# Three one-pass products of split operands in place of sums of fewer fp32 products, in the MLP of a recurrence-plus-MLP kernel

## The chip, the core and the metric

The kernel runs on one core of a Trainium2 chip. The metric is device time in microseconds, the median of the runs. Each core has five engines that work through queues of their own: TensorE (PE, its weight loads shown as PEld), VectorE (DVE), ScalarE (ACT), GpSimd (POOL) and SyncE (SP), which here starts nearly all DMA transfers. TensorE writes only to PSUM, eight banks of 128 x 512 fp32.

## What is computed

```python
def _attn_ref(q, k, v, alpha):            # 4 batches, 8 heads, 768 steps, 48 wide
    ...
    for t in range(S):
        state = alpha[:, :, t, :, None] * state + np.einsum('bhd,bhe->bhde', k[:, :, t], v[:, :, t])
        y[:, :, t] = np.einsum('bhd,bhde->bhe', q[:, :, t], state)
def _moe_ref(x, g_ln, w_ch1, w_ch2):      # x is y as (4, 768, 384)
    ...
    xn = (x - mu) / np.sqrt(var + 1e-06) * g_ln
    ch = np.maximum(xn @ w_ch1, 0.0) @ w_ch2      # 384 -> 1536 -> 384
    return (x + ch).astype(np.float32)
```

The reference's setup multiplies the weights by fp64 factors, so they arrive as 64-bit floats (12 pieces of 768 KB) and are turned into fp32 on the chip.

## The kernel before

**Chunks.** The 768 steps are cut into six chunks of 128 (c = 0 to 5) for each of four batches (b). `attention(c, b)` does the recurrence of one chunk and batch in matrix form: logarithms and exponentials of the sums of alpha (ACT), q and k scaled by them (L312, DVE), transposes on TensorE (L328 in fp32 for c below IN_HALVES = 2, else L349 as 16-bit halves), scores (L369 in chunk 0, L541 else), state updates (L399, L412, L414) and the output (L424 or L440). Then the layer norm: mean and square (L473), x normalised (L479 or L483), x transposed (L490 in fp32, L506 in halves) into xT.

**Weights.** `take_weights(i)` loads piece i (L211), turns it from 64-bit to fp32 with five DVE operations and one of ACT (L223 to L233), and starts the load of piece i + 3. Pieces 0 to 5 are w1, 6 to 11 are w2.

**MLP of chunk 0.** Plain fp32: `hidden` (L564, relu at L567) and `project` (L576).

**MLP of chunks 1 to 5.** A scheme with fewer products, made with sums of blocks, in the manner of Strassen. The first layer needs, for each of two rounds, 15 block products (`hidden_product`, L856, two matmuls of 256 columns each) where a plain one would need 18; the second layer needs 20 (`product`, L676, four matmuls of 192 columns each) where it would need 24. The price is sums: of weights (`combine_first` L805, `combine_weights` L636), of x (`combine_x` L830), of hidden blocks (`combine_hidden` L663), and one or more sums for each product that leaves PSUM (L860 to L899 and L683 to L745, on DVE, ACT, and on POOL as "late" sums such as L692, L881 and L891). The relu is L907 (ACT).

**Order.** The order of the work on all engines is written out by hand: each letter of ORDER takes one more step of one generator. Lower-case letters are `attention` of the 24 chunk-batch pairs, A to L the weight pieces, Y and Z `hidden` and P and Q `project` of chunk 0 (two batches each), M and V the products, S, W, X, N the sums, R the relus, digits loads and the shared matmuls, O the residual input. Each engine does its part in this order and waits where an input or a buffer is not ready.

Of the kernel before, what the change touches and what calls it, by code (L numbers as in the profile page):

```python
# [9 lines left out]
FP32 = mybir.dt.float32  # L10
INT32 = mybir.dt.int32
UINT32 = mybir.dt.uint32
# [7 lines left out]
IN_HALVES = 2  # L20
STAGED = 3

ORDER = (
    "0aa0bb00c2211dd2a3a2aabbbcaaacbbb0bd1a1abbbdfa1dddaaa3bbbec4aac2cd0baaafdAcbe2cc"
    "ffebdddccccdebb31eg0abhAffffeeecA4gdddccA5fdggheddeeeccYYiYhBjfcfhdgeeecggdchhhg"  # L30
    "hBB1ZZZfffB3CCZAefffe5hghB4fCjYYYYYiZZZCYYZZDD2jji3YYiDjjjhiiEZZZC0kDYYY3hhhZEig"
    "FFE5iggjGlF4ZZZZZgglS1lEHYYYhhghHjYYGYYhZZ2llgll3jHZFYGjHkkZkgI0kk0kjjjYZZnKI3i3"
    "ImQSSiiGii4n2jj1jSj5IlkkkkJKSSSSl1feeJn2eKeJLLnhL0hi02jSmPSPSjjmmQ1PPKSSSPkffPP1"
    "fnhPhSmkSWWSQ2SmmSefefWgnggnhQphSogSilllS5n3mimnggXXlXXX33WQQQ0nnXQXk4ppXXomSlll"
    "lnMMpmMoonMMMMMM2MMWSSkk0XSXlmmnnnmmMmMMM3MM13MnMnooppMMMoMMMMWpkrRM0M5poqooo4iq"
    "WWjjMMMMiMMRWMMMpooRiRMMMWMMoMMMlMMOOM1rrr22MMMRRqipMpoiikWMMMMRRMRMMMnnppokMMMM"
    "MRRRNNp3nMONlNlp0nnpWOqtrrmmNWNrN0MMNMMMMMNkNMMMMNN3MMsMMMMMmq0pNlpq1q3kMNOMlkMN"
    "MMMM5XXXXXrrrqq4MqqNXt1XoMMMMMMXXsstqqproM2MrrrJMMuvpoMMMMMMXMMMMMMXsMMMMMtMMrMo"
    "stssMMMqMtMtMM52rrsttssm4ssstMRttMMMMtt1MrMOOMMMMrMvMO2MMMMRRRvRMMMMMMMRRMMRMMML"
    "u31uMMRMRMMssNqNNNvrsmu22RNNNNNRqqNNNNm001MpMMMMMMMMMMM3MMMMMMMMMMMMNMMMrppNoNuv"  # L40
    "vMMoMMMMMXXX3MMM1XXvuu5vuuXvwXXvx4twuuvvqqMXXOOuMMsttttOMMMMMMMMMMXMMMwtMMMMwMMM"
    "33txxxMMMMMMMRqMMMMMMMMMMMMMMMussMsruuwrxRRRMMMMMRRRMRxMMRMMMMwwMMMMMMvxvvvvv5xx"
    "xwwwwwNNRONRRNttqqMMNNxMMMMMxNvMMMMMMMMNNNNNwwxsvMvwwMMxsMMuNNMMXXxNNxxxXXMXXXMM"
    "MXMMMMMXOMMMxMMXXMMMMMMMMMMwwOOuMMMMMMMMMMMMMMMMMMMMMMMMMMMRRRMMMMMMMMMMMROMxwuR"
    "uuwMMMMMMMMMMRRRRNRMMRRMMNMNNMNNNNMMMMMMMMMMMxNMNNXXXXXXMMMXNNMMMMMMNNNMMVVVVVVX"
    "MMMXXXMMMMMMMMVVVVVVVVOOOMOVVVVVVVVVVVVVVVRRRRRVVVVVVVVVRVVVVVVVVVVVVVVVVVVVVVVR"
    "RRNNRNRMMNRNNNMMMNNNMMMMNNNMMMMMMMMMMMMMMMMMMMNNMMMMNMMMMMMMM"
# [4 lines left out]
def kernel(  # L52
# [11 lines left out]

# [10 lines left out]
    NJ = DF // P  # L99
    assert S % P == 0 and H % 2 == 0 and D <= 64 and DM % P == 0 and DF % P == 0  # L100
    assert out.shape == (B, S, DM) and B * P <= 512 and DM + 2 * NP <= 512

    cpool = ctx.enter_context(tc.tile_pool(name="const", bufs=1))
    raw = ctx.enter_context(tc.tile_pool(name="raw", bufs=B // 2))
    stage = ctx.enter_context(tc.tile_pool(name="stage", bufs=STAGED))
# [6 lines left out]

    HS = P // 2
    halves = [slice(HS * s, HS * s + HS) for s in range(2)]
    raws = {}

# [10 lines left out]

    def loads(n):

        src = {"a": alpha, "k": k, "q": q}[n]  # L130
        lone = None
        for c in range(NCB):
            for m in range(B // 2):
                if c < 3:
                    t = raw.tile([P, 2, 2, NP, D], FP32, name=f"r{n}", tag="in", bufs=6)
                elif lone is None:
                    t = lone = raw.tile([P, 2, 2, NP, D], FP32, name=f"r{n}", tag="in", bufs=6)
                step = 2 if 0 < c < 3 else 1
                for i in ((0, 1) if c == 0 else (0,) if step == 2 else (1, 0)):
                    bs = slice(2 * m + i, 2 * m + i + step)  # L140
                    to = t[:, i:i + step].rearrange("t b i p d -> t b (i p d)")
                    if n != "a" or c == 0 or (step == 1 and i == 1):
                        nc.sync.dma_start(
                            to, src[bs, c * P:(c + 1) * P].rearrange("b t h d -> t b (h d)"))
                    else:
                        for h in range(2):
                            nc.sync.dma_start(to[halves[h], :1], of_pair(src, c, m, h)[:, :1])
                        if step == 2:
                            nc.sync.dma_start(to[:, 1], src[2 * m + 1, c * P:(c + 1) * P].rearrange(
                                "t h d -> t (h d)"))  # L150
                    raws.update({(n, c, 2 * m + j): t[:, j] for j in range(i, i + step)})
                    yield

    def loads_of_v():
        for c in range(NCB):
            for m in range(B // 2):
                bs, rows = slice(2 * m, 2 * m + 2), slice(c * P, (c + 1) * P)
                vn = raw.tile([P, 2, 2, NP, D], FP32, name="vn", tag="vn")
# [4 lines left out]
                if c:  # L163

                    vx = raw.tile([P, 2, NP, D], FP32, name="vx", tag="vx")
# [8 lines left out]
    mask, mask_of_halves = tri.bitcast(INT32), consts[:, 2 * P:2 * P + HS].bitcast(INT32)  # L174
# [15 lines left out]

    w1 = cpool.tile([P, NJ // 2, NF, 2 * P], FP32, name="w1")
    w2 = cpool.tile([P, NJ, DM], FP32, name="w2")
# [5 lines left out]
    for i in range(NJ // 2):  # L198
        cs, js = slice(2 * i * P, 2 * (i + 1) * P), slice(2 * i, 2 * (i + 1))
        pieces.append((w1[:, i], w1_src[:, :, cs]))  # L200
        pieces.append((w2[:, js], w2_src[:, js]))
# [770 lines left out]
```

## Time and profile before

| | us |
|---|---|
| median of 3 runs | 424.07 (423.91 to 424.12) |
| span of the profiled execution | 423.5 |
| runs above that span | 0.4 to 0.6 |

The profile does not list a time of its own for the profiled execution; its span, from the first to the last instruction, is what sums are made against, and the runs lie about 0.5 us above it. Busy time is the union of an engine's instructions. PE and PEld records contain a latency that overlaps with the next one, so PE looks busier than its work. Mean granted TensorE clock: 1.000.

### The profile page before, as it was taken

Reading aid. Unit: us, or ns where it says so; the run is one execution under the profiler, and the core shown is the slowest. Engines: PE = TensorE matmul, PEld = TensorE weight load, DVE = VectorE, ACT = ScalarE, POOL = GpSimd, SP = SyncE. Lnnn points to the kernel's source line nnn. Section 1 sums busy time; section 2 is a strip of 40 time slices with the busy share of each in tenths; the row PEclk is TensorE's granted clock in tenths of the full one; section 3 lists DMA queues with packets and bytes.
Section 4 is the critical chain, followed back from the end, with each engine's and each line's share of the span. In section 5 each row is a group of like instructions: output and inputs, shape, how many; then the busy total and the mean of one; then the engine's idle time right before and its main releaser. Section 6 shows DMA issues by size and latency. Waiting matters only on the chain.

```text
span 423.5 us, 14142 instructions
## 1 busy us (share of the span) xinstructions
PE 416.0 (98%) x5988; PEld 366.6 (87%) x5988; DVE 326.9 (77%) x626; ACT 228.0 (54%) x572; POOL 155.2 (37%) x182
## 2 busy tenths in 40 slices
PE   7989999999999999999999999999999999999996
PEld 5878878756778889998889998899998899988996
DVE  3689989898998989778668667749676588756684
ACT  6987577969535879434666066496432541124300
POOL 4242010200116391244671334670145650656414
PEclk9999999999999999999999999999999999999999
DMA  7879866774533341161503136002122000130001
GB/s 234 242 210 276 259 180 187 229 224 146 115 109 122 97 147 45 38 180 30 150 23 111 61 90 159 0 22 39 42 82 70 0 2 0 39 112 2 0 20 56
DMA packets 50791, 43.95 MB, mean 104 GB/s; under 512 B 23164, under 2 KB 46844, under 8 KB 50728
## 3 DMA queue, kind: packets, MB, share of 16 engines
q1 hardware_dynamic: 50696, 43.04, 35.3%
q8 instruction: 47, 0.77, 0.8%
q14 instruction: 16, 0.13, 0.1%
q0 software_dynamic: 32, 0.00, 0.0%
HBM read 34.29 MB, written 8.74 MB: 102 GB/s over the span
## 4 chain that ended last, share of the span: by engine, by line
PE 91%; DVE 3%; DMA 3%; ACT 1%; issue 1%; SPq 1%; DVEq 0%
PE ops L676 31%; PE hps L856 31%; PE ops L576 7%; PE hps L564 7%; PE yps L440 5%; PE aps L541 2%; PE ups L399 2%; PE tps L349 2%; DMA ws<-in_moe_w_ch_dram 2%; PE lps L525 1%; DMA ra<-in_alpha_dram 1%; DVE qk L312 1%; PE xps L506 1%; PE tps L328 1%; PE xps L490 1%
## 5 line engine op out<-in xcount | busy, mean ns | idle before, releaser
L692 POOL TENSOR_TENSOR ob<-ob,u 128x192 f32<-128x192 f32 x40 | 25.5, 648 | 88.5 <-DVE ob L689 66.1
L856 PE MATMUL hps<-sum,w 128*128 128x256 f32 x192 | 47.5, 382 | 0.1
L414 POOL TENSOR_TENSOR mid<-mid,gate 112x192 f32<-112x192 f32 x20 | 10.7, 536 | 92.3 <-DVE mid L412 55.2
L856 PEld LDWEIGHTS hps<-sum,w 128*128 128x128 f32 x192 | 36.1, 190 | 5.1 <-DVE qk L312 0.2
L676 PE MATMUL ops<-w,hT 128*128 128x192 f32 x224 | 39.9, 327 | 0.0
L676 PEld LDWEIGHTS ops<-w,hT 128*128 128x128 f32 x224 | 37.0, 190 | 0.3
L564 PE MATMUL hps<-xT,w 128*128 128x256 f32 x144 | 33.6, 385 | 1.1 <-DVE w L233 0.8
L856 PE MATMUL hps<-xT,w 128*128 128x256 f32 x136 | 34.4, 380 | 0.0
L564 PEld LDWEIGHTS hps<-xT,w 128*128 128x128 f32 x144 | 26.5, 190 | 6.6 <-issue 1.1
L576 PE MATMUL ops<-w,hT 128*128 128x384 f32 x96 | 32.0, 488 | 0.0
L907 ACT ACTIVATE hT<-hT 128x512 f32<-128x512 f32 x48 | 27.3, 629 | 7.8 <-POOL hT L894 2.7
L856 PEld LDWEIGHTS hps<-xT,w 128*128 128x128 f32 x136 | 25.8, 190 | 3.5
L676 PE MATMUL ops<-ws,sum 128*128 128x192 f32 x160 | 28.6, 327 | 0.0
L576 PEld LDWEIGHTS ops<-w,hT 128*128 128x128 f32 x96 | 17.9, 190 | 11.5
L686 DVE TENSOR_TENSOR ob<-ops,ob 128x192 f32<-128x192 f32 x50 | 17.0, 351 | 13.0 <-PE ops L676 7.6
L676 PEld LDWEIGHTS ops<-ws,sum 128*128 128x128 f32 x160 | 26.4, 190 | 0.0
L359 ACT COPY qT<-tps 112x512 uint16<-112x512 uint16 x32 | 17.2, 600 | 16.0 <-PE tps L349 16.0
L676 PE MATMUL ops<-ws,hT 128*128 128x192 f32 x128 | 23.4, 326 | 0.0
L510 ACT COPY xT<-xps 128x384 uint16<-128x384 uint16 x32 | 13.5, 491 | 16.9 <-PE xps L506 16.9
L676 PE MATMUL ops<-more,sum 128*128 128x192 f32 x120 | 22.2, 328 | 0.0
L676 PEld LDWEIGHTS ops<-ws,hT 128*128 128x128 f32 x128 | 21.3, 190 | 0.1
L440 PE MATMUL yps<-mid,qT 48*64 48x48 f32 x320 | 20.9, 220 | 0.0
(254 smaller groups left out, 1138.0 us busy)
## 6 DMA issues: line engine op xcount, KB each, us to landing
ws<-in_moe_w_ch_dram SPq DMA_DIRECT2D x12, 768.0 KB, 5.9
vn<-in_v_dram SPq DMA_DIRECT2D x12, 384.0 KB, 3.9
kept<-x SPq DMA_DIRECT2D x20, 192.0 KB, 2.7
ob<-kept SPq DMA_DIRECT2D x20, 192.0 KB, 2.2
out_dram<-ob SPq DMA_DIRECT2D x19, 192.0 KB, 1.9
rq<-in_q_dram SPq DMA_DIRECT2D x16, 192.0 KB, 4.1
rk<-in_k_dram SPq DMA_DIRECT2D x16, 192.0 KB, 4.3
ra<-in_alpha_dram SPq DMA_DIRECT2D x14, 192.0 KB, 2.5
```

The lines of the kernel that those rows point to most:

```text
L349: nc.tensor.transpose(tv[cs, n, p, w], words[halves[h], n, p, i, :cs.stop - cs.start, w], ident_of_halves[halves[h]])
L359: nc.scalar.copy(out=to, in_=tps[h].bitcast(UINT16).rearrange("r (n p w t) -> r n p t w", n=2, p=NP, w=2)[:R, n])
L414: nc.gpsimd.tensor_mul(new, new, by)
L440: nc.tensor.matmul(yps[r][halves[s], i, p], of, by, start=not (odd and inner), stop=bool(inner or not odd), skip_group_check=bool(odd))
L510: nc.scalar.copy(out=xT_of[c][:, :, b, halves[h]].bitcast(UINT16).rearrange("r f (t w) -> r f t w", w=2), in_=xps[h].bitcast(UINT16)[:, :2 ...
L564: nc.tensor.matmul(hps, w1[:, j // 2, f, j % 2 * P:][:, :P], xT_of[0][:, f, bs], start=(f == 0), stop=(f == NF - 1))
L576: nc.tensor.matmul(ops_of[b], hT_of[c][:, j, b], w2[:, j], start=(j == 0), stop=(j == NJ - 1))
L676: nc.tensor.matmul(acc, lhs[:, j], rhs[:, j], start=(j == 0), stop=(j == NT - 1))
L686: nc.vector.tensor_add(x, acc, x)
L692: getattr(nc.gpsimd, f"tensor_{op}")(x, x, y)
L856: nc.tensor.matmul(acc[:, i], w, b, start=True, stop=True)
L907: nc.scalar.activation(out=x, in_=x, func=AFT.Relu)
```

## The change

For chunks 1 to 5 the block sums go and plain products come. Every fp32 operand is split into a high and a low half, each exact in the 12 bits that the type float32r keeps, and a product of fp32 numbers becomes three products of halves: high by high, low by low (scaled by K = 4096), and a product of two mixed sums. The first two gather in one PSUM bank (pa or the first accumulator), the third in another (pb or the second); the result is the first times 1 + 1/K plus the second.

- The work is cut into ten blocks (chunk, pair of batches) of six steps, one for each piece of w1 and w2. A step is `firsts` (18 matmuls of 256 columns), `scaled` (ACT, out of PSUM), `joined` (DVE, out of PSUM), `highs` (ACT, relu and high half), `lows` (DVE), `mixes` (POOL, two operations of 128x512), `seconds` (12 matmuls of 384 columns). After six steps `results` adds both accumulators of each batch to the residual (DVE, twice 128x384) and sends it.
- Each weight piece is split after it has become fp32: high half on ACT, low half and mixed sum on DVE (128x768 each). g_ln is now multiplied into w1 in the conversion, for chunk 0 as well, instead of by `combine_first` and on chunk 0's x.
- x of chunks 1 to 5 is normalised on DVE instead of ACT, split after its transpose (ACT, DVE) and mixed on POOL (`mix`).
- IN_HALVES goes from 2 to 1: chunk 1 is transposed as 16-bit halves too.
- Buffers are new numbered slots with one owner after another: input tiles one per batch, hidden blocks three deep (slots 18 to 20, the former weight staging), transposed q and k four deep. `project` takes both batches of a pair in one turn, and ORDER is new.

The diff, cut to its core (in the new ORDER M is `firsts`, U `scaled`, T `joined`, R `highs`, V `lows`, W `mixes`, S `seconds`, N `results`):

```diff
+F32R = mybir.dt.float32r
...
-IN_HALVES = 2
+IN_HALVES = 1
 STAGED = 3
+K = 4096.0
+BELOW = 1 - 2.0 ** -13
...
 ORDER = (
...
+    "0a02121ab0abbaaabaacbb00babbcdb3abaf0edCCbbaadbabA2A42ac11bdbcaec1afdbdAa2bcadd1"
+    "c2fcdddf3dffeBafecceadAdebedb5YBc3ff0ef0eCcBeeYh1BgdfcYde4Ycec2hAfhhcd3YYccYffgd"
+    "120dhhCfYecfheggBcAD031ecdAggYgZEDZefeZD25jhhZCgghhY3YEe1iYfZZYeYegE4ejfZFZe2Zgf"
+    "ZfiBhjYEgFhgYDhgZYZYfjei2jBhgfh0iifjgFiZ1jhZGZYZHl0EZ3HYgZYYZiAfYFZH5k4iCiYjFGfj"
+    "ehjijihGkMZ2HUGFij3TPllBZQQlGZPKZ1IiPJjhQPkiQDI2hIMPJQJUFTjRgCEVQQkgKGiIjjgPQijl"
+    "k0PilLPkKLnDHPE0CW1LHkPRmlQh5V3iQPGiD3iIWlkhPIlJMPlUJ4kTPKQlR1nQImnilQlgQ0j1kMLL"
+    "inngUVnhmSK2Tlpg0WhkHknMmUSRgTRVkkMlJSUlWkhjlgO3jTVmmjSRkMUVmlLTOKMU5TRjVWniWmio"
+    "SSmWNnkmjRnNj4mnmm2pV1lMpnNUToWRVSMipUTn1ljNW3nOmkSRpMU2oSTpVlROjMUVMkWWTp0k0UlS"
+    "SolRkTVWnlknnMlkU1RTmoRSVooMVNNqr3NUW4T52orpMmpnkoWRpkVoUTqNpSWmR3SmVorMSopnqUTl"
+    "MorRm2W1OVUWMmUTqRpnopS0TnmrrSrtOVWMRmU0TSRNnonNosNpnqMpVNqVqUpnMUTWT53nqWqpqRqV"
+    "4ootOqqoWrrr1SqtSRVsm2opS3WrMmrpUMTrRmqUTrOoqsopoVtRSM2qqU0qsVMTrW2Uoo0Tr3qtWSRt"
+    "RVsSW2NrtMOsvVpNsNqWU5qt1TuMspRVWtUMUNTrt4sssvT1pptrSRttSVuuS3MrURTVsRrpsOWSWvMU"
+    "SqTMVWU1TuMRVRUvSTNsNRrWuVrursWtNtNtr20stVvMOuSqttvWOv0SSUq3stMTRUVrTWSMRVUTtRVW"
+    "MsU1sWOS5vMSxwsTuuUTvRvRNuNsV43vNWVxuMuMstwvUwUxTu2tOOwvuRxWvTwxVMvUNxsSRSwuWTRv"
+    "VtWxSVStw3WusMtSUsTR5xVwWMvuvMvUSUTTuxwx3wNuRNxRuuVNMMvNwxxVWUTxxUxRwxuTwSwxWVSw"
+    "xRvWwxMUVuTSMxvvURVWTvSWMRUSVWTSRxVMNWOUMMTRVUUNSTwNTwRVwxNRMVWSWwWUTSSwMRUxVwwT"
+    "ORMWVOSWUTSMNURNTRNOMVUTMVUTRWSNMVUWSOWTRVSRVMWUTSWRVSWSNNNN"
 )
...
+    def slot(n, shape, name, dtype=FP32):
+        return one.tile(shape, dtype, name=name, tag=f"s{n}")
...
+    def bank(shape, name):
+        return ps.tile(shape, FP32, name=name, tag="bank", bufs=8)
...
     def take_weights(i):
         if i < STAGED:
             load_weights(i)
             yield
-        if pieces[i][1].dtype != FP32:
...
+        if i == 0:
+            nc.scalar.mul(g_20, g_col, 2.0 ** -20)
+        yield from round_weights(i)
...
+        w = plain_of(i)
+        fine[i] = slot(FINE_AT[i], [P, 2, NF * 2 * P], "wg", F32R)
+        hi, lo = (fine[i][:, n] for n in range(2))
+        nc.scalar.activation(out=hi, in_=w, func=AFT.Copy, scale=BELOW)
+        yield
+        nc.vector.tensor_sub(lo, hi.bitcast(FP32), w)
+        yield
...
+        nc.vector.scalar_tensor_tensor(
+            out=mixed[i // 2][:, i % 2], in0=hi.bitcast(FP32), scalar=-1.0 / K, in1=lo.bitcast(FP32),
+            op0=AOP.mult, op1=AOP.subtract)
...
+        if (c, b // 2) not in xT_of:
+            xT_of[c, b // 2] = one.tile([P, 3, NF, 2, P], F32R, name="xs", tag=f"xs{b // 2}")
+        hi, lo, both = (xT_of[c, b // 2][:, n, :, b % 2] for n in range(3))
+        act(out=hi, in_=xj, func=AFT.Copy, scale=BELOW)
+        yield
+        nc.vector.tensor_sub(lo, xj, hi.bitcast(FP32))
+        yield
+        mix(hi, lo, both)
+        yield
+
+    def mix(hi, lo, both):
+        nc.gpsimd.tensor_scalar(out=lo, in0=lo.bitcast(FP32), scalar1=-K, scalar2=None, op0=AOP.mult)
+        nc.gpsimd.tensor_tensor(out=both, in0=hi.bitcast(FP32), in1=lo.bitcast(FP32), op=AOP.add)
...
+    def project(h, j):
+        w = plain_of(NI + j // 2).rearrange("p (a c) -> p a c", a=2)
+        for b in range(2 * h, 2 * h + 2):
...
-    def combine_weights():
...
-    def combine_hidden(c):
...
-    def product(c, n):
...
-    def combine_first():
...
-    def combine_x(c):
...
-    def hidden_product(c, r, n):
...
-    def relus():
...
+    blocks = [(c, m) for c in range(1, NCB) for m in range(2)]
+    steps = [(n, i) for n in range(len(blocks)) for i in range(NI)]
+    fps_of, u_of, hid_of, acc_of = {}, {}, {}, {}
+
+    def firsts():
+        for n, i in steps:
+            x = xT_of[blocks[n]]
+            pa, pb = bank([P, 2, 2 * P], "pa"), bank([P, 2, 2 * P], "pb")
+            fine_w = fine[i].rearrange("p n (f j) -> p n f j", f=NF)
+            mixed_w = mixed[i // 2][:, i % 2].rearrange("p (f j) -> p f j", f=NF)
+            for r in range(2):
+                for f in range(NF):
+                    for t in range(2):
+                        nc.tensor.matmul(pa[:, r], fine_w[:, t, f, r * P:][:, :P], x[:, t, f],
+                                         start=(f == t == 0), stop=(f == NF - 1 and t == 1))
+            for r in range(2):
+                for f in range(NF):
+                    nc.tensor.matmul(pb[:, r], mixed_w[:, f, r * P:][:, :P], x[:, 2, f],
+                                     start=(f == 0), stop=(f == NF - 1))
+            fps_of[n, i] = pa, pb
+            yield
+
+    def scaled():
+        for key in steps:
+            u_of[key] = work.tile([P, 2, 2 * P], FP32, name="u", tag="u", bufs=2)
+            nc.scalar.activation(out=u_of[key], in_=fps_of[key][0], func=AFT.Copy, scale=1 + 1 / K)
+            yield
+
+    def joined():
+        for key in steps:
+            nc.vector.tensor_add(u_of[key], fps_of[key][1], u_of[key])
+            yield
+
+    def highs():
+        for n, (key, i) in enumerate((s, s[1]) for s in steps):
+            hid_of[key] = slot(18 + n % 3, [P, 3, 2, 2 * P], "hid", F32R)
+            nc.scalar.activation(out=hid_of[key][:, 0], in_=u_of[key], func=AFT.Relu, scale=BELOW)
+            yield
+
+    def lows():
+        for key in steps:
+            hid = hid_of[key]
+            nc.vector.scalar_tensor_tensor(out=hid[:, 1], in0=u_of[key], scalar=0.0,
+                                           in1=hid[:, 0].bitcast(FP32), op0=AOP.max,
+                                           op1=AOP.subtract)
+            yield
+
+    def mixes():
+        for key in steps:
+            mix(*(hid_of[key][:, n] for n in range(3)))
+            yield
+
+    def seconds():
+        for n, i in steps:
+            if i == 0:
+                acc_of[n] = [[bank([P, DM], f"acc{t}") for t in range(2)] for _ in range(2)]
+            hid = hid_of[n, i].rearrange("p n r (b t) -> p n r b t", b=2)
+            fine_w = fine[NI + i].rearrange("p n (r m) -> p n r m", r=2)
+            mixed_w = mixed[NI // 2 + i // 2][:, i % 2].rearrange("p (r m) -> p r m", r=2)
+            for b in range(2):
+                for r in range(2):
+                    for t in range(2):
+                        nc.tensor.matmul(acc_of[n][b][0], hid[:, t, r, b], fine_w[:, t, r],
+                                         start=(i == r == t == 0),
+                                         stop=(i == NI - 1 and r == t == 1))
+            for b in range(2):
+                for r in range(2):
+                    nc.tensor.matmul(acc_of[n][b][1], hid[:, 2, r, b], mixed_w[:, r],
+                                     start=(i == r == 0), stop=(i == NI - 1 and r == 1))
+            yield
+
+    def results():
+        for n, (c, m) in enumerate(blocks):
+            for i in range(2):
+                b = 2 * m + i
+                ob = ob_of[c, b]
+                nc.vector.scalar_tensor_tensor(out=ob, in0=acc_of[n][i][0], scalar=1 + 1 / K,
+                                               in1=ob, op0=AOP.mult, op1=AOP.add)
+                yield
+                nc.vector.tensor_add(ob, acc_of[n][i][1], ob)
+                send(c, b)
+                yield
 ...
-    turns |= {"M": mlp(), "V": hidden_products(NCB - 1), "S": combine_first(), "W": combine_weights(), "R": relus(),
-              "X": (x for c in range(1, NCB) for x in combine_x(c)),
-              "N": (x for c in range(1, NCB) for x in combine_hidden(c)), "O": outputs()}
+    turns |= {"M": firsts(), "U": scaled(), "T": joined(), "R": highs(), "V": lows(), "W": mixes(),
+              "S": seconds(), "N": results(), "O": outputs()}
```

More of the change, by code (lines that the diff above doesn't have):

```diff
@@ L195 @@
+    nc.vector.memset(zero, 0.0)
+    idle = bank([P, 512], "lps")
+    for _ in range(6):
+        nc.tensor.matmul(idle[:, :P], zero, zero, start=True, stop=True)
+    nc.vector.memset(eps, EPS)
+    nc.vector.memset(least, -8.0 * (896 << 20))
     w1_src = w_ch1.rearrange("(f p) j -> p f j", p=P)
     w2_src = w_ch2.rearrange("(j p) m -> p j m", p=P)
-    pieces = []
[L198 to L201, printed above, removed]
@@ new lines, in attention @@
+        yield
+        xj = work.tile([P, NF, P], FP32, name="xj", tag="row", bufs=4)
+        for h in range(2):
+            nc.scalar.copy(out=xj[:, :, halves[h]].bitcast(UINT16).rearrange("r f (t w) -> r f t w", w=2),
+                in_=xps[h].bitcast(UINT16)[:, :2 * NF * HS].rearrange(
+                    "r (f w t) -> r f t w", f=NF, w=2))
+        yield
+        if (c, b // 2) not in xT_of:
+            xT_of[c, b // 2] = one.tile([P, 3, NF, 2, P], F32R, name="xs", tag=f"xs{b // 2}")
```

595 lines of the change are left out of this document (143 added, 452 removed).

## Prediction

> **What bounds the kernel now.** I read the busy table first, then the chain that ended last, then stretches of the span, then the groups by shape. A measurement of this kernel can tell about 0.2% from no change: the three runs lie within 0.05%, and profile and run differ by 0.1%.
>
> The page, busy time and chain:
>
> ```profile
> PE 416.0 (98%) x5988; PEld 366.6 (87%) x5988; DVE 326.9 (77%) x626; ACT 228.0 (54%) x572; POOL 155.2 (37%) x182
> ...
> PE 91%; DVE 3%; DMA 3%; ACT 1%; issue 1%; SPq 1%; DVEq 0%
> PE ops L676 31%; PE hps L856 31%; PE ops L576 7%; PE hps L564 7%; PE yps L440 5%; PE aps L541 2%; PE ups L399 2%; PE tps L349 2%; DMA ws<-in_moe_w_ch_dram 2%; PE lps L525 1%; DMA ra<-in_alpha_dram 1%; DVE qk L312 1%; PE xps L506 1%; PE tps L328 1%; PE xps L490 1%
> ```
>
> TensorE ends the kernel, and 62% of the chain is the two lines that this change replaces. The same span cut in four, at the first L564, at the first L856 and at the last matmul (PE, PEld, DVE, ACT, POOL busy, clock, DMA share, GB/s):
>
> ```profile
> 0.00:30.40 30.40, 26.95 (x442) 21.65 (x442) 18.06 (x41) 24.42 (x60) 11.73 (x26) 1.00 0.79 236
> 30.40:121.30 90.90, 90.60 (x1682) 68.04 (x1682) 83.99 (x143) 64.11 (x159) 10.26 (x17) 1.00 0.68 194
> 121.30:420.30 299.00, 298.44 (x3868) 276.86 (x3864) 224.53 (x443) 139.47 (x356) 133.21 (x139) 1.00 0.22 63
> 420.30:423.50 3.20, 0.00 (x0) 0.00 (x0) 0.36 (x1) 0.00 (x0) 0.00 (x0) 1.00 0.36 120
> ```
>
> From 121.3 to 420.3 us the other engines have room (DVE 75%, ACT 47%, POOL 45%): there PE work taken away is time taken away. Before 121.3 us DVE is 92% busy and the DMA engines 68 to 79%: there PE work taken away may gain nothing.
>
> A matmul's own duration (mean ns) holds a latency that the next one overlaps, so the rate is read from long runs in the chain (start, us, what):
>
> ```profile
> 11.09 2.06 PE aps L369 x32
> ...
> 370.88 23.31 PE hps L856 x108
> 394.19 26.07 PE ops L676 x160
> ```
>
> One fp32 matmul appears as two MATMUL records (L564 has 72 calls and 144 records). L856 at 256 columns takes 215.8 ns per record, L676 at 192 columns 162.9 ns. The means by shape tell the columns' share:
>
> ```profile
> L676 PE MATMUL ops<-w,hT 128*128 128x192 f32 x224 | 39.9, 327 | 0.0
> L676 PEld LDWEIGHTS ops<-w,hT 128*128 128x128 f32 x224 | 37.0, 190 | 0.3
> ...
> L576 PE MATMUL ops<-w,hT 128*128 128x384 f32 x96 | 32.0, 488 | 0.0
> ...
> L541 PE MATMUL aps<-qT,kT 48*64 48x64 f32 x640 | 11.8, 221 | 0.0
> ...
> L349 PE MATMUL tps<-consts,qk 64*64 64x64 bf16 x512 | 10.8, 195 | 0.0
> L541 PEld LDWEIGHTS aps<-qT,kT 48*64 48x64 f32 x640 | 10.5, 134 | 1.6 <-ACT kT L359 1.0 <-issue 0.2 <-ACT la L293 0.2
> ...
> L369 PE MATMUL aps<-qT,kT 48*128 48x128 f32 x64 | 4.2, 279 | 0.0
> ```
>
> From 192 to 384 columns an fp32 record grows by 161 ns, 0.84 ns a column. From 64 to 128 fp32 columns (L541, L369) it is 0.9. The bf16 record at 64 columns lies 26 ns under the fp32 one at 64, so bf16 takes about 0.42 ns a column, half as much. An fp32 record is thus two column passes, and 384 passes cost 162.9 ns, 512 cost 215.8: 0.413 ns a pass and 4 ns fixed.
>
> **The change, part by part.** *Removed on PE*: L856, 5 chunks x 2 x 15 products x 2 matmuls x 2 records = 600 x 0.2158 = 129.5 us; L676, 5 x 20 x 4 x 2 = 800 x 0.1629 = 130.3 us. Together 259.8.
>
> *Added on PE*: 60 steps (ten pairs of batches, six weight pieces). One "firsts" has 18 matmuls of 256 columns, one "seconds" 12 of 384. No fp32r instruction is in this trace. Its bounds are the bf16 row (one pass) and the fp32 record (two passes). I take one pass, since the operands are 12-bit halves and the instruction is meant as one product; 256 passes are 110 ns, 384 are 162.9. So 1080 x 0.110 = 118.8 and 720 x 0.1629 = 117.3, together 236.1: 23.7 us less than before.
>
> *Loads of weights*: 1800 instead of 1400. A 128-column load reads 190 ns (L676) against 134 for 64 columns (L541), about 0.88 ns a column or 112 ns of array. Under L676 it hides in 163 ns. Under a 110 ns matmul it barely does: at L369, with loads of 187 ns and 128-column fp32 records (107 ns of passes), 32 records in two row groups take 2.06 us, 128 ns a record and group. So a firsts matmul costs 110 to 128 ns. I take 110, since fp32r may load in one pass, as the fp32 transposes L490 do (141 ns for 128 columns); the upper end adds 1080 x 0.018 = 19 us.
>
> *Chunk 1's transposes* go from fp32 (L328, 12 in 1.31 us: 32 for 3.5 us; L490, 12 for 1.3 us) to 16-bit halves (L349, 128 in 1.17 us, four times 4.7 us; L506, 72 in 0.71 us, 96 for 0.9): +0.8 us.
>
> *The other engines.* DVE loses the sums of weights, x and hidden blocks (13 x 0.95, 17 x 0.66, 55 x 0.48, 80 x 0.7) and the evictions (120 x 0.685, 120 x 0.35): 230 us. It gains 60 joins (0.69, as L866), 60 lows (0.7, as L663), 40 x 2 result halves (0.55), 20 x (xn and x's low half, 1.1) and, for each of 12 weight pieces, a difference and a mix (0.95 as L636, 0.975 as L233): 173 us. ACT loses about 90 us and gains about 105. POOL loses its late sums (50 x 0.65, 70 x 1.3: 124 us) and gains 80 mixes, each a tensor_scalar and a tensor_tensor. The second is 1.3 us at 128x512 (L881); the first has no row here, between the affine select of that size (0.66, L380) and 1.3. That makes 2.0 to 2.6 us a mix, about 145 to 190 us in all. The Trainium skill's "GPSIMD Engine Reference", section 4.1, holds one-input elementwise work on this engine to be about line rate and two-input work twice as slow as VectorE; the first would be 0.43 us (an estimate), the second the trace shows (1.3 against 0.7), and a mix would be 1.7 us.
>
> Per step PE has 1.98 + 1.95 = 3.9 us, against ACT 1.2, DVE 1.4 and POOL 2.0 to 2.6, so in the late stage no engine passes PE. That is the cover under which I cost them at nothing.
>
> *The first stage* is harder: DVE gets 12 x 1.92 = 23 us more for the split of the weights and ACT 12.3. I added the rows' mean durations along both ORDER strings (such sums count overlap twice: DVE's come to 355 us where the busy table has 327). In the old one the first L856 stands behind 112.8 us of PE, 112.8 of DVE and 105.8 of ACT, and came at 121.3: 8.5 us above PE's sum. After it PE lost nothing (301 us of sum, 299 us of span). In the new one the sixth firsts stands behind 124.6 of PE, 124.2 of DVE, 119.5 of ACT: the same balance, because firsts and chunk 0's second product now overlap. Bytes issued before chunk 0's second product are 18.1 MB against 18.3 for 72 and 69 us of PE work, so the DMA engines bind no sooner. I keep 8.5 us of loss; bounds -6 (11 loads instead of 18 stand before the first weight piece, 7 us on the chain before) and +23 (the split wholly on the path).
>
> *The tail.* Now 3.2 us from the last matmul to the end. After: the last firsts must pass scale 0.59, join 0.69, high 0.63, low 0.7, mix 2.0 to 2.6 = 4.6 to 5.2 us before the last seconds, with two seconds (3.9 us) as cover, and four result operations (2.2 us, half covered) stand where one eviction did. I take +2 us.
>
> Sum against the profiled span: 423.5 - 23.7 + 0.8 + 2 = 402.6 us, and runs lie about 0.5 above the span: 403.
>
> **The rivals.** *A, fp32r is not one pass* (the change doesn't do what it says; the other side). Two passes a column, like each fp32 record, cost 1080 x 0.106 + 720 x 0.159 = 229 us: 632. It decides from 10% above one pass on (23.7 of 236). For it: no row shows the type. Against: exact halves are only worth splitting for a cheaper product. 9%.
> *B, loads bind the firsts* (128 ns): 422, just faster. 8%.
> *C, the weight stage*: the split comes late to firsts and PE waits 10 to 23 us: 413 to 426. For it: DVE is already 92% busy there. 12%.
> *D, PSUM and hand-overs*: four accumulators are held through a block, a step takes two banks, attention two at a time, of eight. A firsts directly behind a firsts (17 of 59 in the new ORDER) may wait for scale and join, 1.3 us, and block ends for results, 1 to 2 us in ten blocks; the shortest leads between firsts and seconds are 3.9 to 8 us of PE work against the 5 us chain. If a quarter to a half of this comes due, 5 to 17 us: 408 to 420. 14%.
> *E, POOL*: behind the first firsts PE has about 5.4 us a step (firsts, seconds and their share of attention) and POOL 0.9 us beside the mix; so a mix over 4.5 us would bind, and one of 5 gives 60 x 5.9 behind a first mix near 115 us, about 470. 7%.
> *F, matmuls overlap more than here*. The Trainium skill, "TensorE: Matmul & The Clock Gate", section Back-to-back issue gap, gives 81 ns at 128 columns and 131 at 512 for streams with loads. Between these, firsts and seconds would take 188 us instead of 236, and the time 355. The trace speaks against it (163 ns for 384 passes). 1%.
> The forecast, 395 to 409, keeps 49%.
>
> **The numbers.** 403 is the likeliest case. 394 to 428 takes in the forecast, B, C and D and leaves out A, E, F and a little more, under 2 in 10. Faster: forecast, D, F, most of B and C: 0.79. Slower: A, E and a little of B and C: 0.19. Same: 0.02.
>
> **What would show it.** Right: seconds in runs at 163 ns, firsts at 110 with loads hidden; PE still over 95% busy behind the first firsts; DVE near 270 us, POOL 180 to 220. Wrong: 216 ns for 256 columns (A), 128 (B); PE idle between 30 and 130 us released by DVE weight rows (C); PE waiting for ACT scale or DVE join and results (D), or for POOL (E).

## The result: slower by 5.7%

448.77 us (median of four runs, 445.35 to 452.88) against 423.99 for the kernel before. The ratio, 1.057 [1.052, 1.062], and the comparisons below leave out a slow run here (452.88) and one in experiment 5 (467.62) and go by the medians of the others, 447.21 and 462.17. The forecast was 403 (394 to 428), so it had the sign wrong. The profiled execution took 447.21 us, its span is 445.5 where the forecast's sum made 402.6, so 42.9 us have to be found.

The page of the changed kernel, busy time and the chain that ended last, by engine and by line:

```profile
PE 421.0 (95%) x6696; PEld 381.2 (86%) x6696; DVE 272.0 (61%) x451; ACT 243.3 (55%) x582; POOL 261.0 (59%) x220
...
PE 83%; DVE 4%; issue 4%; POOL 3%; DMA 3%; ACT 1%; SPq 0%; POOLq 0%; DVEq 0%; ACTq 0%
PE pa L621 17%; PE acc L670 17%; PE pb L625 8%; PE acc L675 8%; PE hps L577 8%; PE ops L590 7%; PE yps L450 4%; PE tps L362 3%; PE ups L410 3%; PE aps L553 2%; POOL hid L527 2%; DMA ws<-in_moe_w_ch_dram 2%; PE lps L538 1%; DMA vn<-in_v_dram 1%; PE xps L507 1%
```

TensorE is busy for 5.0 us more than before (416.0), not 23 less, and idle for 24.5 us instead of 7.5. The share of issue in the chain rose from 1% to 4%. L621 and L625 are the firsts, L670 and L675 the seconds: 50% of the chain, where the two lines that they replace had 62%. The span cut, as before, at the first matmul of chunk 0's hidden layer (L577), at the first firsts (91.8) and at the last matmul (PE, PEld, DVE, ACT, POOL busy, clock, DMA share, GB/s):

```profile
0.00:36.70 36.70, 26.71 (x467) 21.88 (x467) 21.47 (x47) 24.68 (x56) 9.56 (x24) 0.91 0.81 238
36.70:91.80 55.10, 48.79 (x1094) 40.44 (x1090) 42.23 (x77) 41.27 (x106) 16.40 (x12) 0.97 0.59 171
91.80:441.20 349.40, 345.52 (x5144) 318.88 (x5140) 206.98 (x327) 177.39 (x421) 235.01 (x184) 1.00 0.25 73
441.20:445.50 4.30, 0.02 (x1) 0.00 (x0) 1.28 (x3) 0.00 (x0) 0.00 (x0) 0.95 0.25 91
```

Most of the idle time lies ahead of the first firsts, where the granted clock is also below 1; behind it TensorE is 98.9% busy, and the tail is 4.3 us (before 3.2). The chain inside one step (start, us, what):

```profile
214.02 0.72 PE pb L625 x6
214.74 1.39 PE acc L670 x8
216.13 0.69 PE acc L675 x4
```

A firsts matmul of 256 columns takes 120 ns, a seconds one of 384 columns 173.7, where the forecast had 110 and 162.9. TensorE's longest waits:

```profile
PE tps L362 <- issue: 7.3, 4, 3.7
PE tps L341 <- DVE qe L328: 5.1, 1, 5.1
PE yps L450 <- issue: 2.4, 2, 1.3
...
PE acc L670 <- POOL hid L527: 0.9, 2, 0.6
```

L362 are the 16-bit transposes of q and k, L450 the small products behind them. "issue" is time in which an engine waited for nothing that the profile shows. TensorE waits 0.9 us for GpSimd, which rival E feared. The 42.9 us, span against sum:

| term | forecast | measured | difference |
|---|---|---|---|
| products of chunks 1 to 5 | 259.8 to 236.1 | 263.0 to 262.9 | +23.6 |
| idle time of TensorE, tail with it | 7.5 + 2 | 24.5 | +15.0 |
| TensorE's other busy time | +0.8 | +5.1 | +4.3 |

(The measured products are summed from the start of each record to the start of the next, without the idle time between, which was 1.2 us after the change.)

### The profile page after: what moved, and what is told of

It reads as the page before. It is cut to its first block, busy times and chain, and to the rows that moved or that the text cites. A ratio compares the mean times of both kernels' runs of the same rounds, so it can differ in the third digit from the quotient of the medians.

```text
span 445.5 us, 15549 instructions
## 1 busy us (share of the span) xinstructions
PE 421.0 (95%) x6696; PEld 381.2 (86%) x6696; DVE 272.0 (61%) x451; ACT 243.3 (55%) x582; POOL 261.0 (59%) x220
## 4 chain that ended last, share of the span: by engine, by line
PE 83%; DVE 4%; issue 4%; POOL 3%; DMA 3%; ACT 1%; SPq 0%; POOLq 0%; DVEq 0%; ACTq 0%
PE pa L621 17%; PE acc L670 17%; PE pb L625 8%; PE acc L675 8%; PE hps L577 8%; PE ops L590 7%; PE yps L450 4%; PE tps L362 3%; PE ups L410 3%; PE aps L553 2%; POOL hid L527 2%; DMA ws<-in_moe_w_ch_dram 2%; PE lps L538 1%; DMA vn<-in_v_dram 1%; PE xps L507 1%
## 5 line engine op out<-in xcount | busy, mean ns | idle before, releaser
L527 POOL TENSOR_SCALAR hid<-hid 128x512 fp32r<-128x512 f32 x60 | 93.2, 1553 | 73.9 <-DVE hid L650 54.1
L621 PE MATMUL pa<-xs,wg 128*128 128x256 f32 x720 | 97.9, 285 | 0.0
L670 PE MATMUL acc<-wg,hid 128*128 128x384 f32 x480 | 95.9, 339 | 1.0 <-POOL hid L527 0.9
L621 PEld LDWEIGHTS pa<-xs,wg 128*128 128x128 f32 x720 | 91.5, 190 | 2.4 <-DVE mid L423 0.6
L670 PEld LDWEIGHTS acc<-wg,hid 128*128 128x128 f32 x480 | 82.1, 188 | 2.9 <-POOL hid L527 2.2
L528 POOL TENSOR_TENSOR hid<-hid 128x512 fp32r<-128x512 f32 x60 | 79.6, 1327 | 5.0
L650 DVE SCALAR_TENSOR_TENSOR hid<-u,hid 128x512 fp32r<-128x512 f32 x60 | 50.9, 848 | 24.7 <-ACT hid L644 24.3
L625 PE MATMUL pb<-xs,we 128*128 128x256 f32 x360 | 52.9, 283 | 0.0
L675 PE MATMUL acc<-we,hid 128*128 128x384 f32 x240 | 52.0, 337 | 0.0
L625 PEld LDWEIGHTS pb<-xs,we 128*128 128x128 f32 x360 | 47.5, 192 | 0.0
L675 PEld LDWEIGHTS acc<-we,hid 128*128 128x128 f32 x240 | 42.1, 188 | 1.2 <-POOL hid L528 0.8
L577 PE MATMUL hps<-xT,wf 128*128 128x256 f32 x144 | 35.0, 398 | 0.0
L527 POOL TENSOR_SCALAR xs<-xs 128x384 fp32r<-128x384 f32 x20 | 25.4, 1270 | 11.9 <-DVE xs L521 10.6
L577 PEld LDWEIGHTS hps<-xT,wf 128*128 128x128 f32 x144 | 27.8, 198 | 5.0 <-ACT xj L512 0.6
L372 ACT COPY qT<-tps 112x512 uint16<-112x512 uint16 x40 | 23.6, 591 | 13.0 <-PE tps L362 13.0
```

What stands on the lines that cost most here:

```text
L527: nc.gpsimd.tensor_scalar(out=lo, in0=lo.bitcast(FP32), scalar1=-K, scalar2=None, op0=AOP.mult)
L528: nc.gpsimd.tensor_tensor(out=both, in0=hi.bitcast(FP32), in1=lo.bitcast(FP32), op=AOP.add)
L577: nc.tensor.matmul(hps, w[:, f, j % 2 * P:][:, :P], xT_of[0][:, f, bs], start=(f == 0), stop=(f == NF - 1))
L621: nc.tensor.matmul(pa[:, r], fine_w[:, t, f, r * P:][:, :P], x[:, t, f], start=(f == t == 0), stop=(f == NF - 1 and t == 1))
L625: nc.tensor.matmul(pb[:, r], mixed_w[:, f, r * P:][:, :P], x[:, 2, f], start=(f == 0), stop=(f == NF - 1))
L650: nc.vector.scalar_tensor_tensor(out=hid[:, 1], in0=u_of[key], scalar=0.0, in1=hid[:, 0].bitcast(FP32), op0=AOP.max, op1=AOP.subtract)
```

## Experiments

All ratios are to the kernel before, run on the same chip beside them (423.2 to 423.9 us).

**1. Chunk 1's transposes back in fp32.** The theory was that the dense 16-bit transposes run out of instructions.

```diff
+        elif c == 1:
+            both = [bank([R, NP, P], f"tps{i}") for i in range(2)]
...
+                    nc.tensor.transpose(both[i][:, p], qk_of(c, b)[:, i, p]..., ident)
```

> Chunk 1's q and k are transposed in fp32 again (8 matmul records a batch instead of 128), at the same places of ORDER; all else as in the changed kernel (447 us, profile 445.5). Supply theory: TensorE ran out of instructions in the dense 16-bit transposes while the DMA engines were full (16.9 us of 'issue' idle before L362, 1.8 before L349 in the old kernel); then most of the 'issue' idle before 90 us goes, the first firsts comes 4 to 8 us earlier than 91.9 and the time is 439 to 443. Rival, DVE's weight work sets the first stage: the idle only changes its releaser, the first firsts stays within 2 us of 91.9, the time within 2 us of 447.

440.13 us, 1.040 [1.035, 1.044]: 7.1 us came back, and the first firsts came at 84.4 instead of 91.8. The waits of transposes for issue fell from 7.3 to 2.2 us.

**2. The same part alone, in the kernel before.**

```diff
-        if c < IN_HALVES:
+        if c < 1:
```

> The kernel before, with one part of the change alone: chunk 1's transposes of q and k in 16-bit halves (four times 128 short transposes for four times 24 fp32 records). The prediction's price is +0.8 us. Theory (dense short transposes run out of instructions while the DMA engines are full, as in the changed kernel, where fp32 ones gave 8.6 us back): the idle time before them that ends by issue grows from 1.8 us to 6 or more, and the time from 424 to 428 to 432 us. Rival (they starve only where the new order puts them): 424 to 425 us.

431.35 us, 1.018 [1.017, 1.020]: 7.6 us for a part priced at 0.8. (The fp32 transposes leave 8 records a batch, not the 24 of the expectation.) The idle time ahead of the 16-bit transposes, in us and times, before the edit and with it:

```profile
  issue: 1.8, 5
```

```profile
  issue: 11.2, 11
```

This view counts the stops of the weight loads beside those of the matmuls. The matmuls alone had no such stop before the edit and these with it:

```profile
PE tps L349 <- issue: 4.4, 2, 2.3
```

In the changed kernel the chain shows one such stop, in the middle of one batch's transposes:

```profile
50.94 0.50 PE tps L362 x37
51.44 3.67 issue
55.11 0.34 PE tps L362 x17
```

The trace's DMA packets show what comes ahead of its end. The instruction queue q8 moves blocks of 16384 bytes. One started at 52.34 us and landed at 53.64, and TensorE went on at 55.11. So it is at the other stops for issue up to 90 us: landed at 30.20, 47.76 and 78.25, on at 31.79, 49.08 and 79.65; in experiment 1 landed at 70.59, on at 72.01; in this one landed at 24.72 and 40.39, on at 26.44 and 41.82. It is 1.3 to 1.7 us each time. The shortest stop, 0.7 us, ended at 339.0, 1.3 us after a landing. The Trainium skill, "Runtime: NRT & Kernel Launch", section Instruction fetch mechanics, says that instructions come in 16 KiB blocks of 256 over a DMA queue, at a cost "mostly hidden". The blocks are in the trace. At 256 instructions each, the 52 blocks of q8 make 13312, and TensorE's matmuls and loads are 13392, so the blocks are most likely TensorE's. Hidden they are not, where the 128 transposes and 128 loads of one batch use up a block in 1.17 us and a block is 1.0 to 1.4 us under way. Other transfers ran beside it (DMA share 0.81 to 0.94 from 51 to 55 us), but they are not shown to be needed: from 337 to 339 us, around the stop of 0.7 us, the DMA share was 0.00.

The profiled executions of this kernel and of the one before lie 5.5 us apart (429.0 and 423.5): TensorE's idle time grew by 4.5 us, about as much as the new stops make, and its busy time by 1.0. The other 2 us between the medians are not broken down.

**3. The price of a matmul, in place.** Firsts and seconds read the upper 16 bits of the same words as bf16 (so the products are not the reference's); number and shapes stay.

```diff
-nc.tensor.matmul(pa[:, r], fine_w[:, t, f, r * P:][:, :P], x[:, t, f], ...
+nc.tensor.matmul(pa[:, r], half(fine_w[:, t, f, r * P:][:, :P]), half(x[:, t, f]), ...
```

> The matmuls of firsts and seconds read the upper 16 bits of the same operands as bf16 (stepped by two elements); the lower bits are left out, so the products are those of rounded-off numbers; counts and shapes are the same. Rate theory: an fp32r matmul costs 119 ns at 256 columns and 174 at 384 where the column passes give 107 and 160; bf16 takes 110 and 163, PE's work falls by 18 us and the time by 10 to 18, to 429 to 437. Rival, loads and matmuls of any type cost the same here (a weight change in a full array): the times per matmul stay at 119 and 174 and the time within 3 us of 447.

436.01 us, 1.030 [1.025, 1.035]: 11.2 us less than the change. Its chain:

```profile
214.59 0.68 PE pb L631 x6
215.27 1.36 PE acc L676 x8
```

In place a bf16 matmul took 113 and 170 ns, not the 110 and 163 of the expectation, and TensorE's busy time fell by 13.9 us, not 18. The operands are read here at every second element, in experiment 4 side by side; whether that makes the difference was not tested. Even at this price the kernel is 3% slower than before.

**4. The price by itself.** Series of 24 matmuls behind the kernel, in fp32r, fp32 and bf16, and GpSimd's two operations, with fp32r and with fp32 output. It is one run; the granted clock in the series was 1.00.

> Behind the changed kernel's last result stand series of 24 matmuls each into one bank, with 128, 256, 384 and 512 columns, in fp32r, fp32 and bf16, and two in fp32r with the same weights each time; then three of each POOL operation of a mix, 128x512, with fp32r and with fp32 output, while VectorE is idle. Rate theory (a fixed 13 ns an fp32r matmul): 128 columns 110 to 115 ns (load), 256: 119, 384: 174, 512: 226; bf16 56 to 65, 110, 163, 216; fp32 twice the bf16 numbers per call. If the fixed part is the change of weights, the series with the same weights shows 110 and 163. If fp32r is slower per column, 512 shows 230 or more. POOL: if the output type costs, fp32 output is faster than 1.49 us by 0.3 or more; if it is the operation, both are alike, and the sum (1.33) is the cheaper one.

Each fp32 call leaves two records, so a row of 72 is 24 fp32r and 48 fp32 records. TensorE's timeline, then GpSimd's:

```profile
449.23 13.48 PE L707 MATMUL pr<-wg 128*128 128x256 f32 x72
462.55 2.78 PE L707 MATMUL pr<-pb 128*128 128x256 bf16 x24
465.09 19.91 PE L707 MATMUL pr<-wg 128*128 128x384 f32 x72
484.84 4.06 PE L707 MATMUL pr<-pb 128*128 128x384 bf16 x24
```

```profile
440.03 5.62 POOL L728 TENSOR_SCALAR pp<-pp 128x512 fp32r<-128x512 f32 x3
445.74 3.97 POOL L731 TENSOR_TENSOR pp<-pp 128x512 fp32r<-128x512 f32 x3
449.77 4.64 POOL L728 TENSOR_SCALAR pp<-pp 128x512 f32<-128x512 f32 x3
454.49 3.95 POOL L731 TENSOR_TENSOR pp<-pp 128x512 f32<-128x512 f32 x3
```

From start to start, at 128, 256, 384 and 512 columns: fp32r 112, 120, 173.5 and 227 ns; bf16 56, 109, 162 and 216; an fp32 record 112, 216, 322 and 429. So from 256 columns on fp32r makes one pass, but each matmul has some 13 ns beside 0.418 ns a column, where bf16 has about 2. (At 128 columns these would give 67 ns; it took 112.) An fp32 call, two records, costs four times a bf16 one, where the expectation had twice.

As it is the same 13 from 256 to 512 columns, a weight load that outlasts the matmul is not its cause. Two more series, at 256 and 384 columns, used the same weights for all 24 matmuls, loaded again each time, and took 120 and 173 ns as well; so a change of weights is not its cause either. What is was not found. The Trainium skill, "TensorE: Matmul & The Clock Gate", section "Wait — 56ns, not 53.3ns?", gives the time from one matmul to the next as the columns at 2.4 GHz and 2.5 ns; the bf16 series agrees, fp32r does not.

GpSimd's multiplication took 1.49 us and its sum 1.27, with either output, so it is the operation and not the type that costs. (One of the first three multiplications took 2.47, while VectorE was still copying.)

**5. GpSimd's multiplication of the mix on ScalarE.**

```diff
-        nc.gpsimd.tensor_scalar(out=lo, in0=lo.bitcast(FP32), scalar1=-K, ...)
+        nc.scalar.activation(out=lo, in_=lo.bitcast(FP32), func=AFT.Copy, scale=-K)
```

> The multiplication by -K of every mix goes from POOL (1.49 us for 128x512, 1.17 for 128x384) to ScalarE; POOL keeps the sum. POOL theory: PE's waits at 300 to 314, 381 to 388, 411 to 415 and 434 to 439 us, 25 us of chain in all, are POOL's; POOL falls from 261 to about 145 us busy, most of those waits go and the time falls by 8 to 15 us, to 432 to 439. Rival, the waits come from the order of turns (POOL only stood in the chain because something before it was late): PE waits for ScalarE or DVE at the same places and the time stays within 3 us of 447.

462.6 us, 1.091 [1.087, 1.095]: 15 us more (462.17 against 447.21), though GpSimd's busy time fell to 135 us in the first 439. The step now stands behind ScalarE's other work: seconds waited for it six times, 6.0 us in all. The rest of the 15 us is not broken down.

**6. The whole mix of the hidden blocks on VectorE**, in one operation, from experiment 1.

```diff
-            mix(*(hid_of[key][:, n] for n in range(3)))
+            nc.vector.scalar_tensor_tensor(out=both, in0=lo.bitcast(FP32), scalar=-K,
+                                           in1=hi.bitcast(FP32), op0=AOP.mult, op1=AOP.add)
```

> Chunk 1's transposes in fp32 as in the run at 440.1 us, and the mix of the hidden blocks made by VectorE in one operation of about 0.85 us instead of GpSimd's two of 2.88 us; the factor -K sits in the second product's low weights instead (six GpSimd operations more). Theory (GpSimd's two operations make the hand-over from firsts to seconds late): the waits behind the first firsts (6 us) and one or two of the tail's 4.3 us go, 432 to 436 us, GpSimd's busy time falls by about 160 us, VectorE's rises by about 50. Rival 1 (any engine that works in order brings its own queue into the hand-over, as ScalarE did, 462.6 us): 440 to 455. Rival 2 (the late waits are accumulators and PSUM, not the mix): 438 to 441.

The factor -K sits in the second product's low weights instead, which costs six GpSimd operations more. 444.51 us, 1.050 [1.048, 1.052]: the theory fell. GpSimd's busy time went from 259.5 to 104.0 us and the time rose by 4.4, as rival 1 had it, at its lower end. Seconds now waited 2.0 us for VectorE's mix and 1.9 for one of the six new operations, so this run alone does not price the hand-over from GpSimd; experiment 7 does.

**7. No mix at all**, from experiment 1: high x high, high x low and low x high, in as many matmuls of the same shapes (low x low is left out).

```diff
-nc.tensor.matmul(pb[:, r], mixed_w[:, f, ...], x[:, 2, f], ...
+nc.tensor.matmul(pb[:, r], fine_w[:, t, f, ...], x[:, 1 - t, f], ...
```

> The run at 440.1 us (chunk 1's transposes in fp32), with the three products chosen otherwise: high x high, high x low and low x high, in the same number of matmuls of the same shapes, so that no mixed operand is made (80 mixes on GpSimd and 12 on VectorE go; the product of the two low halves is left out). Theory (hand-overs are the small part; only about 1 us of TensorE's idle time ends with GpSimd's hid, and the tail's chain is 2.9 us shorter): 435 to 438. Rival (the mix in GpSimd's queue is what makes the late stage lose 6 us and the tail over 4): 430 to 433. If neither counts, because TensorE is simply busy: 439 to 441.

438.85 us, 1.036 [1.032, 1.041], against 440.13 for experiment 1, within the scatter of both and nearest to the expectation's last case, in which neither counts. Its busy row:

```profile
PE 419.5 (96%) x6472; PEld 381.8 (87%) x6472; DVE 241.3 (55%) x439; ACT 238.0 (54%) x574; POOL 35.4 (8%) x60
```

224 us of GpSimd's work and 29 of VectorE's are gone, and TensorE is as busy as before the edit (419.1).

**8. The early wait.** In experiment 1 TensorE stood for 6.6 us at 17.4:

```profile
PE tps L341 <- DVE qe L328: 6.6, 1, 6.6
```

VectorE had waited for the first weight piece until 17.77 us and then turned two pieces into fp32, with chunk 0's multiplications behind them:

```profile
17.77 0.56 DVE L227 TENSOR_SCALAR wf<-ws 128x768 int32<-128x768 int32 x1 [7.95 <-DMA ws<-in_moe_w_ch_dram]
```

First, the pieces' loads and roundings were moved behind these:

```diff
-...f0edCCbbaadbabA2A42ac11bdbcaec1afdbdAa2bcadd1
+...f0edbbaadbab242ac11CAbdbcaec1afdCAbdAa2bcadd1
```

> Chunk 1's transposes in fp32, and the first two weight pieces' loads and roundings moved behind chunk 0's loads and its second multiplications. Theory (VectorE's early wait for a weight piece holds chunk 0's multiplications of the later batches, 5 to 6 us): the wait of the qe transposes for VectorE goes, the first firsts come 3 to 6 us earlier, 434 to 437 us against 440.1. Rival (the weights are then that much later, and their split sets the first firsts): first firsts as before or later, 440 to 444.

442.65 us, 1.045 [1.044, 1.047], and another wait, longer, in its place:

```profile
PE aps L392 <- DVE kT L346: 9.1, 2, 8.9
```

With experiment 6 added:

> The last two together. If both theories hold and add up: 427 to 432 us, still over the kernel before, since the rate of the fp32r matmuls stays. If only one holds: 433 to 437. If neither: 440 and more.

445.91 us, 1.054 [1.050, 1.059]: neither holds. Next, the roundings behind the evictions of kT too:

```diff
-...11CAbdbcaec1afdCAbdAa2bcadd1c2fcdddf3dffeBafecceadA...
+...11CAbdbcaec1afdbda2bcadd1c2fcdcCAAddf3dffeBafeceadA...
```

> The run at 440.1 us, with the first two weight pieces' roundings moved on VectorE behind the multiplications and the kT evictions of chunk 0's later batches (the run at 442.7 us had moved them behind the multiplications alone, and TensorE then waited 8.9 us for kT). Theory (TensorE's early wait of 6.6 us is VectorE standing before a weight piece with chunk 0's work behind it; it also brings the granted clock down to 0.56 for some us): the wait goes, the clock stays at 1.0, 431 to 434. Rival (the first weights are then later, and the wait comes back before the first matmuls of chunk 0's hidden layer): 438 to 443.

442.48 us, 1.046 [1.042, 1.050]: 4.4 us of waiting for kT and 3.0 for chunk 1's qk. With experiment 7 added:

> The last two together. If the theories add up: 427 to 431, still slower than the kernel before (424), since TensorE's busy time stays at 417 to 419 us where the kernel before has 416. If it came below 424, the price of the fp32r matmuls would not be what keeps the change from gaining.

441.45 us, 1.043 [1.040, 1.047]. Then the pieces' loads behind eighteen others, as in the kernel before:

```diff
-...ac11CAbdbcaec1afdbda2bcadd1c2fcdcCAAddf3dffeBafeceadAdebedb5YBc3...
+...ac11bdbcaec1afdbda2bcadd1c2fcdcddf3ACdffeBafeAACceadAdebedb5Bc3...
```

> The run at 440.1 us, with the loads of the first two weight pieces issued behind the first eighteen loads of q, k, alpha and v (chunk 1's first among them, as in the kernel before) instead of behind eleven, their roundings behind chunk 1's first multiplications, and the hidden layer's first step of chunk 0 a little later. The two earlier moves left 9 us of TensorE's idle time between 17 and 28 us and only changed what it waited for (kT, then chunk 1's qk). Theory (TensorE has no other work there because the weight pieces, 1.5 MB, are loaded ahead of chunk 1's inputs): the idle time before the first 30 us falls from 9 to about 2 us as in the kernel before, the granted clock stays at 1.0, 430 to 434. Rival (the bytes in all set this stage, whatever their order): the idle time moves behind to the hidden layer's first steps, 438 to 443.

443.99 us, 1.048 [1.042, 1.053]: kT 4.1, vn's DMA 1.9, VectorE ahead of the hidden layer 1.3. Then the stretch from 15 to 30 us written anew, chunk 0's chain first in every queue:

```diff
+...112123CAbadcdcdddcccdcdcefdcdcdcffeefeffeedcAACdcbababadcBaAbab5Y...
```

> The run at 440.1 us, with the whole stretch of the order from 15 to 30 us written anew: the second half of chunk 0's chain (multiplications, transposes, evictions of qT and kT, products) stands first in every queue, VectorE's, ScalarE's and TensorE's, and the normalisation of the first half, chunk 1's exponentials and the first weights' rounding follow. In the last three orders another operation stood ahead of that chain each time (a weight's rounding, then xn and ScalarE's exponentials ahead of the evictions). Theory (the 9 us are the sum of what in-order queues have ahead of chunk 0's chain): idle time before 30 us 3 to 5 us instead of 9, first firsts 79 to 81 us instead of 84.4, 433 to 437 us. Rival (this stage has its time from the loads and the chain's own length): 438 to 444.

442.96 us, 1.046 [1.041, 1.050]. TensorE came to 27.6 us with 1.6 us idle since 13, and then stood:

```profile
PE xps L503 <- DVE xn L497: 5.6, 1, 5.6
```

With experiment 7 added:

> The same with the three products high x high, high x low and low x high (no mixed operands, the product of the low halves left out): all that the runs so far suggest, in one kernel. Theory (TensorE's own work, 418 to 419 us busy against 416 before, is what keeps it from gaining): 431 to 436 us, over 424 in any case. If it came below 424, waits and not TensorE's work would decide.

440.87 us, 1.042 [1.037, 1.047]. Here ScalarE stood before a weight piece with xn's means behind it; its step went behind them:

```diff
-...123CAbad...dcAACdcbababadcBaAbab5Y...
+...123ACbad...dcAdcbabaAbadcBabAabC5Y...
```

> The last order (443.0 us) with ScalarE's step of the first weight piece moved behind the normalisation of chunk 0's first half: in that run TensorE came to 27.6 us with under 3 us of idle time after the start, and then waited 5.6 us for xn, because ScalarE stood before the weight piece with xn's means behind it. Theory (the 9 us are one operation that waits for a weight piece at the head of an in-order queue, wherever it is put, and go when nothing of chunk 0 stands behind it): 4 to 5 us less idle time before 40 us, clock 1.0, first firsts at 79 to 81 us, 434 to 437 us. Rival (the time is set by when the weight pieces have landed, since TensorE then comes to the hidden layer that much earlier): the wait moves to the hidden layer's first step, 439 to 444 us.

443.12 us, 1.046 [1.043, 1.049]: the waits for xn fell to 3.2 us (2.6 at 27.6 and 0.6 at 43.6), and others of 0.8 and 0.6 followed at 39 and 51. With experiment 7 added:

> The same with the three products high x high, high x low, low x high and no mixed operands: by the theory 432 to 435 us, by the rival 438 to 442; above 424 by both, since TensorE's busy time stays at 418 us or more and no order gives it back.

442.17 us, 1.043 [1.037, 1.048].

So all five theories fell, and the time lay in the rival's range four times (the third order's 443.99 us is above it). The three runs with experiment 7 added missed their theories too. The first firsts came at 84.4 us in experiment 1 and at 86.7, 85.4, 84.3, 86.2 and 86.7 in the five orders, and TensorE's idle time up to 90 us was 10.6 and 12.9, 11.1, 11.3, 11.4 and 10.4. With each move another late operation stood at the head of an engine's queue. What fixes the sum, the loads or the chain's own length, stays open. Once the transposes are in fp32, no order tried is faster than the change's own.

## Why the prediction was wrong, step by step

**The price of firsts and seconds (110 and 162.9 ns) was mis-sized**, and that takes 18.6 of the gain's 23.7 us. Both were taken from fp32 records at one pass, with their 4 ns fixed; fp32r has 13. 1080 x 0.120 + 720 x 0.1737 = 254.7 us, 18.6 more than forecast. What lies between such records takes the other 5.0: it was 3.2 us before (263.0 against the 259.8 of the sum) and 8.2 after (262.9 against 254.7), and the sum had left it out on both sides. A saving of 23.7 us was 0.1. Rival A had named the point from which it decides, 10% over one pass; 18.6 of 236.1 is 8%, and with the time between records it is 11%. Its two passes did not come, nor rival B's 128 ns.

**"Chunk 1's transposes: +0.8" was 7 to 8 us.** The sum priced the transposes by their time in long runs and left out that 512 of them and their loads, in place of 32 and theirs, have to be fetched. Experiments 1 and 2 give 7.1 and 7.6 us, from both sides.

**"I keep 8.5 us of loss" ahead of the first firsts failed.** The sixth firsts, expected at 124.6 + 8.5 = 133 us, came at 149.1, behind 132.8 us of TensorE's busy time and 16.3 of idle time. Idle time up to 90 us was 16.3 us against 3.7 up to 90 before. Some of it is the transposes; with these undone 10.6 are left. Rival C had the place, TensorE waiting in the early stretch for VectorE at a weight piece (5.1 us), though what stood behind the piece was chunk 0's own multiplication, not the split. The bound from below there (-6, since only 11 loads stand ahead of the first piece) did not come. That these pieces come ahead of chunk 1's inputs may have cost time instead, but it is not shown: the third order of experiment 8 puts their loads back and gains nothing. Two readings behind this term were off as well. The 8.5 us were not all idle time in the kernel before: up to the first L856, at 121.3 us, TensorE was busy for 117.6 us, where the rows added up made 112.8. And VectorE's 92% holds from 30.4 us on; over the 121.3 us it is 84%.

**TensorE's other busy time** rose by 5.1 us instead of 0.8. Four stretches behind stops of TensorE show a likely reason (PE busy, granted clock, DMA share, GB/s):

```profile
20.00:24.00 4.00, 1.51 (x8) 0.73 0.82 257
24.00:28.00 4.00, 3.62 (x90) 0.84 0.96 292
...
32.00:36.00 4.00, 4.00 (x82) 0.57 0.83 264
...
56.00:60.00 4.00, 4.00 (x13) 0.58 1.02 235
```

Busy time by the missing clock is 0.4 + 0.6 + 1.7 + 1.7 = 4.4 us. The Trainium skill, "TensorE: Matmul & The Clock Gate", section "What's actually happening", has the clock halved after an idle window of about 3.4 us; the lower clock at 20 to 28 and at 56 to 60 us follows idle times of 5.1 and 3.7 us, which agrees. That at 32 to 36 us follows one of only 1.5 us (30.3 to 31.8), and in the third order of experiment 8 a clock of 0.57 at 295 to 299 us follows one of 1.8; that does not agree. After stops of 1.1 and 1.4 us, at 48 and 78 us, the clock stayed at 1.00. The kernel before has 1.00 in its first 40 us.

**The mix** was 1.55 + 1.33 = 2.88 us, over the forecast's 2.0 to 2.6, and GpSimd had 261 us instead of 180 to 220:

```profile
L527 POOL TENSOR_SCALAR hid<-hid 128x512 fp32r<-128x512 f32 x60 | 93.2, 1553 | 73.9 <-DVE hid L650 54.1 <-ACT hid L644 6.3 <-PE yps L450 4.1
L528 POOL TENSOR_TENSOR hid<-hid 128x512 fp32r<-128x512 f32 x60 | 79.6, 1327 | 5.0
```

What the prediction weighed from the Trainium skill's "GPSIMD Engine Reference", section 4.1 (one-input work at line rate), does not agree: the one-input operation is the dearer one, with VectorE idle too (experiment 4). But the step that cost it at nothing held: TensorE waits 0.9 us for it, and experiment 7 took it away and gained nothing clear of the scatter. Rivals D, E and F did not come: behind the first firsts TensorE was idle for 3.9 us in all, and no product was cheaper than forecast.

**Right** were one pass a column, VectorE near 270 us (272.0), TensorE over 95% busy behind the first firsts (98.9%) and, nearly, the tail (+1.1 for +2). They did not decide.

## What to carry to other kernels

Where a change replaces the work of the bounding engine by 9% less of another kind, the whole gain hangs on the unknown rate: a fixed 9 ns more a matmul, times 1800, was most of it, so the rate's error belongs in the sum and not with the unlikely rivals. Count instructions as well as columns: many tiny ones in a row have to be fetched, and TensorE can stand waiting for that. And a wait at the head of an engine's queue was not won back here by moving it, before it was known what came late next.

## What the runs showed of the hardware

From 256 columns on, fp32r needs one pass a column and about 13 ns a matmul beside it (120 ns at 256 columns, 227 at 512; bf16 109 and 216); at 128 columns it took 112 ns. TensorE's stops for issue, 0.7 to 3.7 us at a time in the changed kernel, ended 1.3 to 1.7 us after a 16 KB block of instructions had landed. GpSimd's tensor_scalar of 128x512 (1.49 us median) costs more than its tensor_tensor (1.29). Idle times of TensorE of 1.5, 3.7 and 5.1 us were paid for twice, the second time by a granted clock of 0.57 to 0.84 in the stretch behind them; stops of 1.1 and 1.4 us were not. How many bits fp32r keeps, 12 by the change's own split, no run here measures.
